# Attention decode over a long cache: scores and P V on TensorE in blocks of three pieces instead of piece by piece

## The chip, the core and the metric

The kernel runs on one core of one Trainium2 chip. The metric is the device time of one launch in microseconds (us). Most of the work is a stream of 512 MB of K and V out of HBM that TensorE (PE), VectorE (DVE) and the DMA queues share.

## The reference, cut to what matters

```python
xn = _layernorm(x)                                   # x: 4 x 1 x 512
q = (xn @ wq) -> (B=4, H=32, 1, Dh=128)
scores = einsum("bhqd,bhkd->bhqk", q, k_cache) * Dh ** -0.5   # k_cache: 4 x 32 x 8192 x 128
p = softmax(scores)
o = einsum("bhqk,bhkd->bhqd", p, v_cache)                     # v_cache: 4 x 32 x 8192 x 128
out = x + o @ wo + (silu(xn @ w_gate) * (xn @ w_up)) @ w_down
```

All tensors are bfloat16. One query per sequence meets 8192 keys in each of 128 pairs of sequence and head.

## The kernel before

The 128 pairs are cut into 32 tiles of four heads of one sequence. A tile's K and its V are 128 partitions x 32768 bf16 each (8.39 MB), and each fills one of three big buffers called slots. `load_k` (L94) and `load_v`/`v_from` (L107) issue one DMA for a whole slot on SyncE's queue (SP), and the issue waits until the slot's last reader is done. The order of all work is written out by hand, with no scheduler.

Scores of a tile come in NP = 32 pieces. For piece p, `t_piece` (L278) lets DVE transpose part of K out of the slot into a small buffer `kt`, of which there are three; `s_piece` then runs two matmuls (`sps<-kt,zq`, 128 weight columns, 512 columns streamed). After the last piece come `max_1` (L291, DVE) and `build_q` for the next tile (L269, DVE). The softmax of tile i-1 is finished inside tile i: `max_2` (L297 to L306) at piece 4, `row_sums` at piece 14, and `pt_turn` (L315), which turns the probabilities into the weights `ptz`, at piece 18. P V of a tile is 64 chunks, each one matmul `oacc<-slot,ptz` with 16 weight columns and 512 columns of V (`pv_chunk`). All these matmuls go through the helper `mm` and so carry L75.

Side by side means this: in the first half of tile i (16 pieces), P V of tile i-2 does its second 32 chunks, and in the second half P V of tile i-1 does its first 32. `pieces` yields after each piece, and the loop then calls `pv_to(n, k)`, which runs chunks until k of tile n are done. Two slots come free on the way: V of tile i-2 at the end of the first half, where `load_k(i + 1)` stands, and K of tile i at its last transpose, where `load_v(i)` stands. Every fourth tile also does `fin` of a group of heads between its last piece and the next tile's first (seven such tiles in the steady part). The last tile (n = 31) has no half of that kind: its 32 pieces run beside all 64 chunks of tile 30.

Of the kernel before, what the change touches and what calls it, by code (L numbers as in the profile page):

```python
# [15 lines left out]
def kernel(  # L16
# [61 lines left out]
    def slot():  # L78
        return slots.tile([P, SLOT], dt.bfloat16, name="slot")
# [11 lines left out]
    def load_k(n):  # L91
        j, b = divmod(n, B)
        t_ = slot()
        nc.sync.dma_start(out=t_[:], in_=A_k_cache[b, j * HT:(j + 1) * HT, :, :].rearrange("h (p t) d -> (h p) (t d)", t=T))  # L94
        k_tiles[n] = t_

    def load_v(n, parts=(T,)):
        t_ = slot()
        v_from(n, t_, 0, 0, parts)

    def v_from(n, t_, base, t0, parts):

        j, b = divmod(n, B)
        src = A_v_cache[b, j * HT:(j + 1) * HT, :, :].rearrange("h (p t) d -> (h p) (t d)", t=T)
        v_tiles[n, t0 * Dh] = (t_, base)
        for w in parts:
            nc.sync.dma_start(out=t_[:, base:base + w * Dh], in_=src[:, t0 * Dh:(t0 + w) * Dh])  # L107
            base, t0 = base + w * Dh, t0 + w
# [106 lines left out]
    def load_ffn():  # L215
        t_ = slot()
        w, w3 = EC * F, 2 * EC * F + FC * D
        nc.sync.dma_start(out=t_[:, 0:w], in_=B_w_gate.rearrange("(p c) f -> p (c f)", c=EC))
        nc.sync.dma_start(out=t_[:, w:2 * w], in_=B_w_up.rearrange("(p c) f -> p (c f)", c=EC))
        nc.sync.dma_start(out=t_[:, 2 * w:w3], in_=B_w_down.rearrange("(p c) e -> p (c e)", c=FC))  # L220
        ffn["w"] = (t_[:, 0:w].rearrange("p (c f) -> p c f", c=EC),
                    t_[:, w:2 * w].rearrange("p (c f) -> p c f", c=EC),
                    t_[:, 2 * w:w3].rearrange("p (c e) -> p c e", c=FC))

    def do_ffn():
        wg, wu, wd = ffn["w"]

        gu_ps = psM.tile([P, 2, FC * B], dt.float32, name="mps")
        for i, w in enumerate((wg, wu)):
            for fc in range(FC):  # L230
                for c in range(EC):
                    mm(gu_ps[:, i, fc * B:(fc + 1) * B], w[:, c, fc:F:FC], xnt_w[:, c, 0:B],
                       start=(i == 0 and fc == 0 and c == 0))
        eg = kt_pool.tile([P, FC * B], dt.float32, name="kt")
        nc.scalar.activation(out=eg[:], in_=gu_ps[:, 0, :], func=ACT.Exp, scale=-1.0)
        nc.vector.tensor_scalar(out=eg[:], in0=eg[:], scalar1=1.0, scalar2=None, op0=ALU.add)
        sig = kt_pool.tile([P, FC * B], dt.float32, name="kt")
        nc.vector.reciprocal(out=sig[:], in_=eg[:])
        gs = kt_pool.tile([P, FC * B], dt.float32, name="kt")
        nc.vector.tensor_tensor(out=gs[:], in0=gu_ps[:, 0, :], in1=sig[:], op=ALU.mult)  # L240
        ht = kt_pool.tile([P, FC * B], dt.bfloat16, name="kt")
        nc.vector.tensor_tensor(out=ht[:], in0=gs[:], in1=gu_ps[:, 1, :], op=ALU.mult)
        for fc in range(FC):
            for half in range(2):
                mm(yo_ps[half][0:B, :], ht[:, fc * B:(fc + 1) * B], wd[:, fc, half * DH:(half + 1) * DH], start=False)
# [18 lines left out]
    def build_q(n):  # L264
        j, b = divmod(n, B)
        for a in range(NQ):
            h = j * HT + a
            half, cg, hh = h // 16, (h % 16) // 4, h % 4
            nc.vector.tensor_copy(  # L269
                out=zq[a * QB:(a + 1) * QB, :, XO + a * QB].rearrange("p (j r) -> p r j", r=2),  # L270
                in_=qt[a * QB:(a + 1) * QB, half, :, hh * 2:hh * 2 + 2, cg * B + b])
# [17 lines left out]
    def max_1(n):  # L289
        mx = small.tile([P, 1], dt.float32, name="mx")  # L290
        nc.vector.reduce_max(out=mx[:], in_=s_ps[n][:], axis=AX.X)  # L291
        nmx[n] = mx

    def max_2(n):

        mps = psM.tile([P, 512], dt.float32, name="mps")
        nc.tensor.matmul(mps[:, 0:P], lhsT=nmx.pop(n)[:, 0:1].to_broadcast([P, P]), rhs=ident_f[:, :],  # L297
                         is_transpose=True, start=True, stop=True, skip_group_check=True)
        nm = small.tile([P, HT], dt.float32, name="nm")
        nc.vector.tensor_reduce(out=nm[:], in_=by_row(mps[:, 0:P]), axis=AX.X, op=ALU.max, negate=True)  # L300
        nc.vector.tensor_tensor(out=nm[:], in0=nm[:], in1=rowb_q[:], op=ALU.mult)  # L301
        nb = small.tile([P, 1], dt.float32, name="nb")
        nc.vector.reduce_sum(out=nb[:], in_=nm[:], axis=AX.X)
        p_ = pp.tile([P, 512], dt.bfloat16, name="p_")
        rs = small.tile([P, 1], dt.float32, name="rs")
        nc.scalar.activation(out=p_[:], in_=s_ps.pop(n)[:], func=ACT.Exp, bias=nb[:, 0:1], scale=qscale,  # L306
                             accum_out=rs[:])
        pt[n] = p_
        rs_t[n] = (rs, mps)

    def pt_turn(n):
        p_ = pt[n]
        t_ = ptz
        for y in range(HT):
            nc.vector.transpose(out=t_[y * QB:(y + 1) * QB, :, y, :, :].rearrange("p s u x -> p s (u x)"),  # L315
                                in_=p_[y * QB:(y + 1) * QB, :].rearrange("p (s w) -> p s w", s=4))
        pt[n] = t_[:].rearrange("p s y u x -> p (s y u x)")

    def row_sums(n):
        j, b = divmod(n, B)  # L320
        rs, mps = rs_t.pop(n)
        mm(mps[:, P:P + HT], rs[:, 0:1].to_broadcast([P, P]), rowb[:], start=True)
        if b == 0:
            rcp[j] = small.tile([P, HT, B], dt.float32, name="rcp")
        nc.vector.reciprocal(out=rcp[j][:, :, b], in_=mps[:, P:P + HT])  # L325
# [5 lines left out]
    def pv_chunk(n, k):  # L331
        j, b = divmod(n, B)
        w = HT * NV
        off = p_off(k)
        mm(o_acc[j % 2][b * QB:b * QB + w, :], pt[n][:, off:off + (w - 1) * QB + 1:QB],
           v_cols(n, k * 512, (k + 1) * 512), start=(k == 0))
# [18 lines left out]
    def x_tile():  # L355
        return psX.tile([P, HT, B], dt.float32, name="xps")
# [21 lines left out]

    NK = T // NV
    NP = 2 * NTG  # L380
    JL = H // HT - 1
    KM = 24
    TL = 48
# [10 lines left out]
    def pv_to(n, k):  # L394
        while pv_at[n] < k:
            pv_chunk(n, pv_at[n])
            pv_at[n] += 1

    def pieces(n, p0, p1):
        for p in range(p0, p1):  # L400
            t_piece(n, *divmod(p, 2))
            s_piece(n, *divmod(p, 2))
            yield p - p0 + 1

    def fin(n):
        nonlocal wo_ready
        j, b = divmod(n, B)
        if b == B - 1:
            fin_1(j)
            fin_q(j)  # L410
            wo_ready = (j + 1) * HT

    HP = NP // 2
    build_q(0)
    load_v(0)
    for i in range(NT - 1):

        for p in pieces(i, 0, HP):
            if i >= 3:
                pv_to(i - 2, NK // 2 + 2 * p)  # L420
            if i != 2 and i > 0:
                if p == 4:
                    max_2(i - 1)
                if p == HP - 2:
                    row_sums(i - 1)
        if i >= 3:
            load_k(i + 1)

        for p in pieces(i, HP, NP):
            if p == 2 and i > 0:  # L430
                pt_turn(i - 1)
            if i >= 2 and p > 2:
                pv_to(i - 1, (p - 2) * (NK // 2) // (HP - 2))

        if i == 0:
            load_ffn()
        elif i == 1:
            load_k(2)
        elif i == NT - 2:
            load_v(i, (T // 4,) * 4)  # L440
        else:
            load_v(i)
        max_1(i)
        build_q(i + 1)
        if i >= 3:
            fin(i - 2)
        if i == 1:
            pv_to(0, 8)
            max_2(1)
            pv_to(0, NK)  # L450
            row_sums(1)
            load_v(1)
            do_ffn()
            load_k(3)

    n = NT - 1
# [7 lines left out]
    v_from(n, t_, H * D, 0, (T // 4, T // 4))  # L464
    for p in pieces(n, 0, NP):
        if p == 4:
            pt_turn(n - 1)
        if p > 8:
            pv_to(n - 1, (p - 8) * NK // (NP - 8))
    t_ = slot()  # L470
    v_from(n, t_, 0, T // 2, (64, 32, 16, 8, 8))
    max_1(n)
# [5 lines left out]
    pv_to(n, KM)  # L478
    fin_1(JL)
    xps = x_tile()  # L480
    pv_last(xps, KM * NV, T - TL, start=True)
    fin_2(JL, xps)
    pv_last(xps, T - TL, T)
    fin_3(JL, xps)
    wo_ready = H
# [38 lines left out]
```

## Time and profile before

| | |
|---|---|
| three runs | 1495.29, 1498.81, 1510.18 us; median 1498.81 |
| the profiled execution | 1507.21 us, its span 1505.4 us, mean granted PE clock 0.931 |
| PE busy | 1242.3 us (83%) |
| DVE busy | 858.5 us (57%) |
| HBM read | 550.77 MB, 366 GB/s over the span |

A busy share says how long an engine had something in flight, not whether it was on the path that sets the end. That is read from the chain of waits and, tile by tile, from the timeline.

### The profile page before, as it was taken

How to read it: one execution, taken by the hardware profiler on the slowest of the kernel's cores; microseconds unless marked ns; L12 is line 12 of the kernel's file. 1: busy time of each engine (PE TensorE's matmuls, PEld its weight loads, DVE VectorE, ACT ScalarE, POOL GpSimd, SP SyncE). 2: the span in 40 equal slices, each digit the busy share in tenths (PEclk: the TensorE clock that was granted, in tenths of full speed). 3: DMA queues.
4: the chain of work that ended last, by engine and by line, in shares of the span. 5: the costliest groups of instructions: out<-in, count | busy, mean ns of one | idle time of the engine just before them, and what ended most of it. 6: DMA issues, size and time to landing. Idle time of an engine off the chain costs nothing.

```text
span 1505.4 us, 12238 instructions
## 1 busy us (share of the span) xinstructions
PE 1242.3 (83%) x4812; PEld 322.9 (21%) x4812; DVE 858.5 (57%) x1509; ACT 34.9 (2%) x79; POOL 3.6 (0%) x11
## 2 busy tenths in 40 slices
PE   2898878888888888878888788788897888888899
PEld 1251212211122112221112211122121211212124
DVE  4935656555565555565556555566555555555553
ACT  1000000000000000000000000000000000000000
POOL 0000000000000000000000000000000000000000
PEclk9889989999999999999999899999999889998899
DMA  9999888988897988978988789887899778898794
GB/s 418 420 435 433 352 348 363 391 362 363 363 389 337 417 363 364 391 333 361 420 347 351 309 363 418 377 347 309 363 391 420 333 305 340 387 417 347 296 414 201
DMA packets 12609, 551.55 MB, mean 366 GB/s; under 512 B 1276, under 2 KB 1800, under 8 KB 3080
## 3 DMA queue, kind: packets, MB, share of 16 engines
q1 hardware_dynamic: 12536, 550.77, 86.2%
q8 instruction: 37, 0.61, 0.1%
q14 instruction: 20, 0.16, 0.0%
q10 hardware_dynamic: 16, 0.01, 0.0%
HBM read 550.77 MB, written 0.00 MB: 366 GB/s over the span
## 4 chain that ended last, share of the span: by engine, by line
PE 60%; DMA 28%; DVE 10%; issue 2%; DVEq 0%; ACT 0%; SPq 0%
PE sps L75 29%; DMA slot<-in_A_k_cache_dram 28%; PE oacc L75 27%; DVE kt L278 5%; DVE ptz L315 2%; PE mps L75 1%; PE xps L75 1%; PE yo_ps L75 1%; PE mps L297 1%; DVE mx L291 1%; DVE o L352 0%; DVE zq L269 0%; DVE nm L300 0%; DVE rcp L325 0%; DVE nm L301 0%
## 5 line engine op out<-in xcount | busy, mean ns | idle before, releaser
L75 PE MATMUL sps<-kt,zq 128*128 128x512 bf16 x2048 | 669.6, 414 | 226.0 <-DVE kt L278 226.0
L278 DVE STREAM_TRANSPOSE kt<-slot 128x512 uint32<-128x512 uint32 x1024 | 679.6, 694 | 253.2 <-PE sps L75 209.6
L75 PE MATMUL oacc<-slot,ptz 128*16 128x512 bf16 x2008 | 630.7, 407 | 1.5 <-DMA slot<-in_A_v_cache_dram 1.5
L75 PEld LDWEIGHTS <-zq 128*128 128x128 bf16 x2048 | 141.2, 100 | 658.1 <-issue 598.1
L75 PEld LDWEIGHTS <-ptz 128*16 128x16 bf16 x2008 | 144.7, 111 | 452.1 <-issue 425.4
L300 DVE TENSOR_REDUCE nm<-mps 128x4 f32<-128x64 f32 x32 | 7.2, 225 | 131.0 <-PE mps L297 131.0
L325 DVE RECIPROCAL rcp<-mps 128x4 f32<-128x4 f32 x32 | 5.9, 185 | 115.5 <-PE mps L75 115.5
L291 DVE TENSOR_REDUCE mx<-sps 128x1 f32<-128x512 f32 x32 | 22.1, 691 | 86.1 <-PE sps L75 86.1
L75 PE MATMUL xps<-rowy,o 128*32 128x4 f32 (+1 forms) x226 | 10.5, 204 | 16.9 <-DVE o L352 16.9
L269 DVE COPY zq<-qt 32x4 bf16<-32x4 bf16 x128 | 21.2, 165 | 1.3
L75 PEld LDWEIGHTS xps<-rowy,o 128*32 128x32 f32 (+1 forms) x226 | 9.8, 154 | 20.3 <-DVE o L352 20.3
L75 PEld LDWEIGHTS <-slot 128*128 128x128 bf16 (+1 forms) x306 | 12.5, 120 | 5.7 <-DVE slot L198 2.6
L75 PEld LDWEIGHTS mps<-rowb,rs 128*128 128x128 f32 x64 | 9.6, 187 | 12.8 <-issue 12.6
L75 PE MATMUL mps<-rowb,rs 128*128 128x4 f32 x64 | 12.2, 261 | 0.0
L297 PE MATMUL mps<-ident_f,mx 128*128 128x128 f32 x32 | 10.4, 325 | 0.0
L349 ACT COPY kt<-oacc 128x512 f32<-128x512 f32 x8 | 4.7, 585 | 238.4 <-PE sps L75 228.5
L350 DVE TENSOR_TENSOR kt<-kt,rowu 128x512 f32<-128x512 f32 x8 | 5.5, 692 | 5.9 <-ACT kt L349 5.7
L372 DVE TENSOR_TENSOR otn<-xps,rcp 32x16 bf16<-32x16 f32 x28 | 4.8, 170 | 7.2 <-PE xps L75 5.2
L75 PE MATMUL yo_ps<-slot,otn 128*4 128x256 bf16 x64 | 8.3, 290 | 0.3 <-DVE otn L362 0.3
L352 DVE TENSOR_REDUCE o<-kt 128x128 f32<-128x512 f32 x8 | 8.2, 1022 | 0.3
L297 PEld LDWEIGHTS mps<-ident_f,mx 128*128 128x128 f32 x32 | 4.3, 136 | 13.2 <-issue 12.3
L75 PE MATMUL sps<-slot,xnt_w 128*32 128x512 bf16 x32 | 3.6, 630 | 4.3 <-DMA slot<-in_A_wq_dram 4.3
(148 smaller groups left out, 182.8 us busy)
## 6 DMA issues: line engine op xcount, KB each, us to landing
slot<-in_A_v_cache_dram SPq DMA_DIRECT2D x7, 2048.0 KB, 16.3
slot<-in_A_wq_dram SPq DMA_DIRECT2D x1, 4096.0 KB
slot<-in_A_wo_dram SPq DMA_DIRECT2D x1, 3584.0 KB, 23.0
slot<-in_B_w_gate_dram SPq DMA_DIRECT2D x1, 1792.0 KB, 24.2
slot<-in_B_w_up_dram SPq DMA_DIRECT2D x1, 1792.0 KB, 28.1
slot<-in_B_w_down_dram SPq DMA_DIRECT2D x1, 1792.0 KB, 32.1
slot<-in_A_v_cache_dram SPq DMA_DIRECT2D x1, 1024.0 KB, 10.5
slot<-in_A_k_cache_dram SPq DMA_DIRECT2D x32, 22.6
```

Source lines behind the costliest of these rows:

```text
L75: nc.tensor.matmul(out_ap, lhsT=lhsT, rhs=rhs, start=start, stop=True, skip_group_check=True, **kw)
L269: nc.vector.tensor_copy(out=zq[a * QB:(a + 1) * QB, :, XO + a * QB].rearrange("p (j r) -> p r j", r=2), in_=qt[a * QB:(a + 1) * QB, half, ...
L278: nc.vector.transpose(out=kt[:].bitcast(dt.uint32).rearrange("p (t r) -> p t r", r=QB), in_=src[:, :, jb, :])
L291: nc.vector.reduce_max(out=mx[:], in_=s_ps[n][:], axis=AX.X)
L297: nc.tensor.matmul(mps[:, 0:P], lhsT=nmx.pop(n)[:, 0:1].to_broadcast([P, P]), rhs=ident_f[:, :], is_transpose=True, start=True, stop=True, ...
L300: nc.vector.tensor_reduce(out=nm[:], in_=by_row(mps[:, 0:P]), axis=AX.X, op=ALU.max, negate=True)
L315: nc.vector.transpose(out=t_[y * QB:(y + 1) * QB, :, y, :, :].rearrange("p s u x -> p s (u x)"), in_=p_[y * QB:(y + 1) * QB, :].rearrange( ...
L325: nc.vector.reciprocal(out=rcp[j][:, :, b], in_=mps[:, P:P + HT])
L349: nc.scalar.copy(out=o_sb[:].rearrange("p u d -> p (u d)"), in_=o_acc[j % 2][:])
L350: nc.vector.tensor_tensor(out=o_sb[:], in0=o_sb[:], in1=rowu[:].unsqueeze(2).to_broadcast([P, NV, Dh]), op=ALU.mult)
L352: nc.vector.reduce_sum(out=o1[:], in_=o_sb[:].rearrange("p u d -> p d u"), axis=AX.X)
L372: nc.vector.tensor_tensor(out=otn[q0:q1, j * 4:j * 4 + 4, :], in0=xps[q0:q1], in1=r_[q0:q1, y, :].unsqueeze(1).to_broadcast([QB, 4, B]), o ...
```

## The change

After each piece the old code ran two or three chunks of P V. The new code does that only after each third piece (PB = 3), and then runs six or seven chunks in the first half of a tile, eight in the second half, and nine or ten in the last tile. The number of pieces, chunks and matmuls and the order of DVE's, ScalarE's and SP's instructions stay. In the first half the last chunk now stands behind piece 15 instead of 16; in the second half the first chunk stands behind piece 22 (the sixth) instead of 19 (the third); in the last tile behind piece 12 instead of 9.

```diff
+    PB = 3
     for p in pieces(i, 0, HP):
-            if i >= 3:
-                pv_to(i - 2, NK // 2 + 2 * p)
+            if i >= 3 and p % PB == 0:
+                pv_to(i - 2, NK // 2 + p * (NK // 2) // (HP - HP % PB))
...
     for p in pieces(i, HP, NP):
-            if i >= 2 and p > 2:
-                pv_to(i - 1, (p - 2) * (NK // 2) // (HP - 2))
+            if i >= 2 and p > PB and p % PB == 0:
+                pv_to(i - 1, (p - PB) * (NK // 2) // (HP - HP % PB - PB))
...
     for p in pieces(n, 0, NP):
-        if p > 8:
-            pv_to(n - 1, (p - 8) * NK // (NP - 8))
+        if p > 3 * PB and p % PB == 0:
+            pv_to(n - 1, (p - 3 * PB) * NK // (NP - NP % PB - 3 * PB))
```

PE at `max_2` in the first half of a tile, before: `kt_3444` holds piece 4 and `kt_3460` piece 5 of the scores; `ptz_129` are the weights of P V.

```order
L75 MATMUL sps_3427<-kt_3444,zq_111 128x512
L75 LDWEIGHTS ptz_129
L75 MATMUL oacc1_116<-slot_3171,ptz_129 16x512
L75 LDWEIGHTS ptz_129
L75 MATMUL oacc1_116<-slot_3171,ptz_129 16x512
L297 MATMUL mps_3450<-ident_f_106,mx_3393 128x128
L75 LDWEIGHTS zq_111
L75 MATMUL sps_3427<-kt_3460,zq_111 128x512
```

The same place after the change, where `kt_3458` is piece 5 and `kt_3462` piece 6:

```order
L75 MATMUL sps_3427<-kt_3444,zq_111 128x512
L297 MATMUL mps_3448<-ident_f_106,mx_3393 128x128
L75 LDWEIGHTS zq_111
L75 MATMUL sps_3427<-kt_3458,zq_111 128x512
L75 LDWEIGHTS zq_111
L75 MATMUL sps_3427<-kt_3458,zq_111 128x512
L75 LDWEIGHTS zq_111
L75 MATMUL sps_3427<-kt_3462,zq_111 128x512
L75 LDWEIGHTS zq_111
L75 MATMUL sps_3427<-kt_3462,zq_111 128x512
L75 LDWEIGHTS ptz_129
L75 MATMUL oacc1_116<-slot_3171,ptz_129 16x512
```

The chunks that stood ahead of `max_2` and behind piece 5 have moved behind piece 6.

PE at the end of the same first half, before: `kt_3528` is piece 16, `kt_3536` piece 17, and the second `oacc1` matmul is the last reader of the slot that `load_k` waits for.

```order
L75 MATMUL sps_3427<-kt_3528,zq_111 128x512
L75 LDWEIGHTS ptz_129
L75 MATMUL oacc1_116<-slot_3171,ptz_129 16x512
L75 LDWEIGHTS ptz_129
L75 MATMUL oacc1_116<-slot_3171,ptz_129 16x512
L75 LDWEIGHTS zq_111
L75 MATMUL sps_3427<-kt_3536,zq_111 128x512
```

The same place after the change, where `kt_3530` is piece 16:

```order
L75 MATMUL oacc1_116<-slot_3171,ptz_129 16x512
L75 LDWEIGHTS ptz_129
L75 MATMUL oacc1_116<-slot_3171,ptz_129 16x512
L75 LDWEIGHTS zq_111
L75 MATMUL sps_3427<-kt_3530,zq_111 128x512
L75 LDWEIGHTS zq_111
L75 MATMUL sps_3427<-kt_3530,zq_111 128x512
L75 LDWEIGHTS zq_111
L75 MATMUL sps_3427<-kt_3536,zq_111 128x512
```

The slot's last reader now stands ahead of piece 16.

## Rows read from the trace of the kernel before

**Rows 1.** The page's part 4: the chain that ended last, by engine.

```profile
PE 60%; DMA 28%; DVE 10%; issue 2%; DVEq 0%; ACT 0%; SPq 0%
```

**Rows 2.** Timeline of SP: start us, duration us, then the DMA issued (28 L94 rows, 166.96 to 1414.93).

```profile
166.96 0.33 SPq L94 DMA_DIRECT2D slot<-in_A_k_cache_dram  x1
...
439.77 0.33 SPq L94 DMA_DIRECT2D slot<-in_A_k_cache_dram  x1
...
713.66 0.33 SPq L94 DMA_DIRECT2D slot<-in_A_k_cache_dram  x1
731.74 0.33 SPq L107 DMA_DIRECT2D slot<-in_A_v_cache_dram  x1
759.54 0.33 SPq L94 DMA_DIRECT2D slot<-in_A_k_cache_dram  x1
...
1176.27 0.33 SPq L94 DMA_DIRECT2D slot<-in_A_k_cache_dram  x1
...
1414.93 0.33 SPq L94 DMA_DIRECT2D slot<-in_A_k_cache_dram  x1
```

**Rows 3.** Chain of waits in order of time: start us, us, what it ran through.

```profile
418.36 0.72 DVE kt L278
...
459.16 0.69 DVE mx L291
...
900.65 21.71 DMA slot<-in_A_k_cache_dram
```

**Rows 4.** Timeline, all engines, 713 to 760: start, us, engine, [idle before <-releaser].

```profile
713.56 1.08 PE L75 MATMUL sps<-kt,zq 128*128 128x512 bf16 x4
...
722.18 0.63 PE L75 MATMUL sps<-kt,zq 128*128 128x512 bf16 x2
...
722.84 0.71 DVE L278 STREAM_TRANSPOSE kt<-slot 128x512 uint32<-128x512 uint32 x1 [0.69 <-PE sps L75]
...
725.16 0.62 PE L75 MATMUL oacc<-slot,ptz 128*16 128x512 bf16 x2
...
725.71 0.62 PE L75 MATMUL sps<-kt,zq 128*128 128x512 bf16 x2
...
726.26 0.83 PE L75 MATMUL oacc<-slot,ptz 128*16 128x512 bf16 x3
...
727.03 0.62 PE L75 MATMUL sps<-kt,zq 128*128 128x512 bf16 x2
...
736.70 2.49 DVE L278 STREAM_TRANSPOSE kt<-slot 128x512 uint32<-128x512 uint32 x4 [0.86 <-DMA slot<-in_A_k_cache_dram]
```

**Rows 5.** Timeline of tile 1: P V with no scores in between.

```profile
83.46 12.27 PE L75 MATMUL oacc<-slot,ptz 128*16 128x512 bf16 x56
```

**Rows 6.** The page's part 5, weight loads: count | busy us, mean ns | idle before.

```profile
L75 PEld LDWEIGHTS <-zq 128*128 128x128 bf16 x2048 | 141.2, 100 | 658.1 <-issue 598.1
L75 PEld LDWEIGHTS <-ptz 128*16 128x16 bf16 x2008 | 144.7, 111 | 452.1 <-issue 425.4
```

**Rows 7.** Timeline of PE, 396 to 490: the piece after `pt_turn`.

```profile
443.49 0.61 PE L75 MATMUL sps<-kt,zq 128*128 128x512 bf16 x2 [2.75 <-DVE kt L278]
```

**Rows 8.** Windows: length, busy of PE, PEld, DVE, ACT, POOL, PEclk, DMA share, GB/s.

```profile
740.00:741.00 1.00, 1.00 (x3) 0.13 (x2) 0.00 (x0) 0.00 (x0) 0.00 (x0) 0.50 0.45 197
...
759.00:760.00 1.00, 1.00 (x5) 0.33 (x5) 0.38 (x1) 0.00 (x0) 0.00 (x0) 1.00 0.00 0
...
100.00:150.00 50.00, 41.05 (x191) 14.35 (x190) 28.09 (x49) 0.22 (x1) 0.00 (x0) 0.86 1.01 435
```

**Rows 9.** Timeline, start of another tile, after a longer wait of PE.

```profile
1152.40 2.53 DVE L278 STREAM_TRANSPOSE kt<-slot 128x512 uint32<-128x512 uint32 x4 [2.81 <-DMA slot<-in_A_k_cache_dram]
1153.16 1.01 PE L75 MATMUL sps<-kt,zq 128*128 128x512 bf16 x2 [4.16 <-DVE kt L278]
```

**Rows 10.** Timelines of PE and of DVE, last tile: piece 5 on, and its maximum.

```profile
1450.06 4.42 PE L75 MATMUL sps<-kt,zq 128*128 128x512 bf16 x10 [2.86 <-DVE kt L278]
...
1483.80 0.69 DVE L291 TENSOR_REDUCE mx<-sps 128x1 f32<-128x512 f32 x1 [3.03 <-PE sps L75]
```

## The prediction

> **What bounds the kernel now.** I read the chain of waits first. PE holds 60% of it and DMA 28% [rows 1], so neither alone is the bound, and the question is where each sits. SP's timeline answers that: a tile's beat is the time from one K issue to the next, and the 28 steady issues give (1414.93 - 166.96) / 27 = 46.2 us [rows 2]. The reader should lay one beat out. K for the next tile is issued at 713.66, when PE has read the last chunk of the old V; it lands at 736.70, where DVE's first transpose had waited for nothing else [rows 2, 4]. That is 23.0 us; the shortest load on the chain took 21.7 [rows 3]. Then comes the first half of the new tile, 736.70 to 759.54, 22.8 us, at whose end the last P V chunk frees the slot for the next K. So the beat is K's load plus a first half on PE. The second half runs inside K's load and the V load inside the first half; both have slack. In the last microsecond before the K issue at 759.54 the DMA moved nothing [rows 8], so it is PE that holds the transfer back there, not bandwidth. At the best rate seen, 435 GB/s [rows 8], K and V of a tile (2 x 8.39 MB) need 38.6 us, well under 46.2.
>
> In seven tiles of the 28, the ones with a `fin`, the second half is longer than K's load and takes its place in the beat. In five others there is no wait for K either, but by fractions of a microsecond.
>
> What PE pays within a half: a pair of score matmuls and a pair of P V chunks take turns and each pair costs 0.55 us, 725.16 to 725.71 to 726.26 [rows 4]. A third chunk in a row adds only 0.77 - 0.55 = 0.22, and a run of 56 chunks cost 12.27 / 56 = 0.22 each [rows 4, 5]. Two further score matmuls in a row add 1.08 - 0.62 = 0.46, so 0.23 each [rows 4]. A piece with two chunks, 1.10 us, is thus 0.23 + 0.22 for the second of each pair and 0.65 for the two turns from one kind to the other. If a turn cost no more than a matmul in a run, those 0.65 would be 0.45.
>
> **The change, part by part.** *First half.* The turns go from 16 rounds to 5. Before: 16 pieces with two chunks, 16 x 1.10 = 17.6 us. After, a block of three pieces and six chunks is 5 x 0.23 + 5 x 0.22 + 0.65 = 2.90 us; five of them and two more chunks are 14.9, and K's issue no longer stands behind piece 16. That is 2.7 less. Against it: the first three pieces of a tile have no chunks between them, so DVE paces them, at 2.49 / 4 = 0.62 a piece [rows 4] instead of the 0.46 that PE needs, 2 x 0.16 = 0.3. After `max_2` DVE starts afresh behind its small reductions, which PE waits for now as then; but piece 6 follows piece 5 without chunks between, another 0.16. `row_sums` stalls PE as before. Net 2.2 us a half, and 28 halves give 62 us.
>
> *Can DVE feed the blocks?* It may start a transpose when a `kt` buffer is read: it started 0.66 us after the piece's first matmul (722.18 to 722.84) and took 0.71 [rows 4]. In a block starting at 0 the three buffers come free at about 0.66, 1.12 and 1.58, the transposes end by 1.4, 2.0 and 2.6, and PE wants the first at 2.90. So it costs nothing, with 0.3 us of cover for the third and 1.5 for the first.
>
> *Second half.* Up to piece 19 nothing moves: PE waits for `pt_turn` as before. From piece 19 to the maximum the trace has 443.49 to 459.16, 15.7 us [rows 3, 7]. After: pieces 19 to 22 at DVE's pace 3 x 0.62 = 1.9, piece 22 with eight chunks and two turns 0.23 + 7 x 0.22 + 0.65 = 2.4, three blocks of three pieces and eight chunks 3 x 3.34 = 10.0, and 0.7 from piece 32's start to the maximum: 15.0. The 0.7 saved counts in the seven `fin` tiles, 5 us, and in part in the five without a wait, 2 us; in the other sixteen K's load covers it and PE only waits longer.
>
> *Last tile.* Piece 5 to the maximum is 1450.06 to 1483.80, 33.7 us, of which five pieces ran at 4.42 / 5 = 0.88 [rows 10]. After: seven pieces at 0.88, 6.2; piece 12 with nine chunks 2.6; five blocks with nine chunks 17.8; one with ten 3.8; pieces 31 and 32 with the way to the maximum 1.1: 31.5. With the second half ahead of it, 3 us.
>
> *Clock.* This is where the change can lose. [...] A deeper fall is on record: after 4.16 us of waiting the clock was low from the first matmul, and the half ran from 1152.40 to 1176.27, 23.9 [rows 2, 9]. If twenty more halves did that it would cost 20 x 1.0 = 20 us. Bounds 0 and 20; I take 0, because the low stretch falls on pieces that DVE now paces, where it costs 0.88 - 0.62 = 0.26 a piece; two scores and two chunks at half the clock would lose up to 4 x 0.22.
>
> *Sum.* 62 + 5 + 2 + 3 - 7 = 65 us. The profiled execution took 1507.2 (span 1505.4) and would take 1442; it lies 8 us above the median of the three runs, 1498.8, and from there I forecast **1434 us**, 4.3% less.
>
> [...]
>
> **Rivals.** *DVE starves the blocks (slower).* Three buffers, three pieces: if DVE could refill only behind the block's chunks, at about 2.6 us, the first piece would be ready at 3.3 and the next two 0.62 apart, so the next block's scores would end at 3.3 + 1.24 + 0.46 = 5.0 instead of 2.90 + 3 x 0.46 = 4.3, 0.7 a block and 3.5 a half. From 2.2 / 5 = 0.44 a block on the kernel is slower; at 0.7 it is 28 x 1.3 = 36 us slower, 1535. Against it: the start 0.66 after the first matmul of a piece. 4%.
>
> *The DMA takes the gain (no change).* If the loads ran no faster than today's average, K would land later by what the first half saves, and the beat would stay at 46.2: 1499. For it: the beat would fall to 43.9, of which 38.6 is the floor. Against it: the idle DMA ahead of a K issue. 5%.
>
> *Weight loads come into the open (slower).* The loads take 0.10 and 0.11 us [rows 6]. A first half has 25 gaps between two scores and 27 between two chunks: 25 x 0.10 + 27 x 0.11 = 5.5 us, against the 2.2 gained, 3.3 x 28 = 92 us, 1591. Against it: 0.22 and 0.23 in runs of 56 and 4 leave no room for a load in the open. 2%.
>
> *The clock falls deeper.* With the 20 us above, 45 us are left, 1454; still faster. 8%.
>
> **How the numbers follow.** The forecast has 80%, and with the clock's rival 88% lie below 1484. A measurement of this kernel can tell about 1% from no change; 6% is within it, 5 for the DMA and 1 for a mixture, and 6% slower. The range takes the clock's 20 us and another 10 for prices read too well (0.01 us in a matmul of a run is 0.5 us a half, 15 in all) at the high end: 1464. At the low end K's loads may come down to the 21.7 of the shortest, about 1 us in sixteen tiles, and the five halves may keep their clock, with some more from the runs: 31 us, 1403.
>
> **What would show it.** The timeline of the changed kernel should have runs of six score matmuls and of six to eight chunks, a block of 2.9 us in the first half, no wait of PE for DVE inside such a block, and the three waits at `max_2`, `row_sums` and `pt_turn` as before. From K's landing to the next K issue it should take 19 to 21 us, from a K issue to the landing 22 to 23, and the beat 43 to 44. PE's wait ahead of a tile should grow, and the granted clock be low at the start of nearly every tile. I am wrong if the runs of scores cost more than 0.25 a matmul, if DVE's starts come behind the chunks, if the low clock lasts past `max_2`, or if K's load grows by what the half gains.

## The result, and the profile after

The changed kernel takes 1423.12 us (median; 1421.55 to 1424.33) against 1498.83: ratio 0.948, 95% interval [0.943, 0.953], 76 us less. The forecast was 1434. The profiled execution took 1422.08.

The page of the changed kernel: span, busy time, and the chain that ended last by engine.

```profile
span 1420.3 us, 12185 instructions
...
PE 1120.2 (79%) x4730; PEld 425.3 (30%) x4812; DVE 822.0 (58%) x1509; ACT 34.9 (2%) x79; POOL 3.6 (0%) x11
...
PE 50%; DMA 36%; DVE 10%; issue 3%; another core or an unknown queue 1%; DVEq 0%; ACT 0%; SPq 0%
```

PE's share of the chain fell from 60% [rows 1] to 50% and the DMA's rose from 28% to 36%: the beat is still K's load plus a first half on PE, but the second term shrank. Some score matmuls have no record in this trace (1966 of 2048 have one), so that a run of six can show as five; whether the 1% of the chain under "another core or an unknown queue" comes of that is open.

SP's timeline, first and last steady K issue and one beat:

```profile
163.54 0.33 SPq L94 DMA_DIRECT2D slot<-in_A_k_cache_dram  x1
...
381.74 0.33 SPq L94 DMA_DIRECT2D slot<-in_A_k_cache_dram  x1
398.93 0.33 SPq L107 DMA_DIRECT2D slot<-in_A_v_cache_dram  x1
422.51 0.33 SPq L94 DMA_DIRECT2D slot<-in_A_k_cache_dram  x1
...
1336.22 0.33 SPq L94 DMA_DIRECT2D slot<-in_A_k_cache_dram  x1
```

The mean beat is (1336.22 - 163.54) / 27 = 43.4 us, against 46.2 [rows 2]. PE's timeline in the first half that ends at 422.51, one whose clock stayed up (its first transpose began at 403.72):

```profile
404.48 1.80 PE L75 MATMUL sps<-kt,zq 128*128 128x512 bf16 x6 [3.02 <-DVE kt L278]
406.21 1.48 PE L75 MATMUL oacc<-slot,ptz 128*16 128x512 bf16 x6
407.62 0.62 PE L75 MATMUL sps<-kt,zq 128*128 128x512 bf16 x2
408.09 0.27 PE L297 MATMUL mps<-ident_f,mx 128*128 128x128 f32 x1
409.68 1.20 PE L75 MATMUL sps<-kt,zq 128*128 128x512 bf16 x4 [1.32 <-DVE kt L278]
410.81 1.48 PE L75 MATMUL oacc<-slot,ptz 128*16 128x512 bf16 x6
412.23 1.52 PE L75 MATMUL sps<-kt,zq 128*128 128x512 bf16 x5
413.68 1.70 PE L75 MATMUL oacc<-slot,ptz 128*16 128x512 bf16 x7
415.31 1.53 PE L75 MATMUL sps<-kt,zq 128*128 128x512 bf16 x6
416.77 1.48 PE L75 MATMUL oacc<-slot,ptz 128*16 128x512 bf16 x6
418.18 1.07 PE L75 MATMUL sps<-kt,zq 128*128 128x512 bf16 x4
```

A block of three pieces and six chunks runs from 415.31 to 418.18, 2.87 us, with no wait inside it; piece by piece, three pieces took three times 1.10 [rows 4]. The half is 422.51 - 403.72 = 18.8 us, against 21.4 for the same kind before [rows 2, 3].

Most halves are not of that kind. The windows of a first half that began with a low clock (columns as in [rows 8]) and the first row of PE in it:

```profile
319.00:321.00 2.00, 2.00 (x6) 0.58 (x4) 1.56 (x3) 0.00 (x0) 0.00 (x0) 0.50 1.21 524
321.00:323.00 2.00, 2.00 (x6) 0.55 (x5) 0.00 (x0) 0.00 (x0) 0.00 (x0) 0.50 1.21 524
404.00:406.00 2.00, 1.52 (x6) 0.48 (x5) 2.00 (x4) 0.00 (x0) 0.00 (x0) 1.00 1.21 524
```

```profile
318.80 2.72 PE L75 MATMUL sps<-kt,zq 128*128 128x512 bf16 x6 [2.83 <-DVE kt L278]
```

The granted clock is 0.50 there and 1.00 at 404; the half with the low clock took 21.3 us. Of the 28 halves 3 kept their clock, that is, it stayed at 1.00 from the first transpose to the K issue (5 before).

### The profile page after: what moved, and what is told of

Same layout as the page of the kernel before. It is cut to its first block, busy times and chain, and to the rows that moved or that the text cites. A ratio compares the mean times of both kernels' runs of the same rounds, so it can differ in the third digit from the quotient of the medians.

```text
span 1420.3 us, 12185 instructions
## 1 busy us (share of the span) xinstructions
PE 1120.2 (79%) x4730; PEld 425.3 (30%) x4812; DVE 822.0 (58%) x1509; ACT 34.9 (2%) x79; POOL 3.6 (0%) x11
## 4 chain that ended last, share of the span: by engine, by line
PE 50%; DMA 36%; DVE 10%; issue 3%; another core or an unknown queue 1%; DVEq 0%; ACT 0%; SPq 0%
DMA slot<-in_A_k_cache_dram 36%; PE sps L75 24%; PE oacc L75 23%; DVE kt L278 5%; DVE ptz L315 1%; PE xps L75 1%; PE yo_ps L75 1%; PE mps L75 1%; DVE o L352 1%; DVE nm L300 0%; DVE rcp L325 0%; DVE mx L291 0%; PE mps L297 0%; DVE nm L301 0%
## 5 line engine op out<-in xcount | busy, mean ns | idle before, releaser
L278 DVE STREAM_TRANSPOSE kt<-slot 128x512 uint32<-128x512 uint32 x1024 | 643.2, 682 | 268.8 <-PE sps L75 170.1
L75 PE MATMUL sps<-kt,zq 128*128 128x512 bf16 x1966 | 591.0, 418 | 257.4 <-DVE kt L278 253.5
L75 PE MATMUL oacc<-slot,ptz 128*16 128x512 bf16 x2008 | 515.2, 401 | 0.5 <-issue 0.5
L75 PEld LDWEIGHTS <-zq 128*128 128x128 bf16 x2048 | 187.1, 102 | 612.4 <-issue 426.4
L75 PEld LDWEIGHTS <-ptz 128*16 128x16 bf16 x2008 | 194.3, 109 | 317.5 <-issue 169.5
L75 PE MATMUL xps<-rowy,o 128*32 128x4 f32 (+1 forms) x226 | 10.7, 205 | 22.9 <-DVE o L352 22.9
L75 PE MATMUL mps<-rowb,rs 128*128 128x4 f32 x64 | 9.3, 215 | 0.1
L75 PE MATMUL mps<-xnt_w,slot 128*128 128x4 bf16 x112 | 6.8, 199 | 0.3 <-DVE rcp L325 0.3
## 6 DMA issues: line engine op xcount, KB each, us to landing
slot<-in_B_w_gate_dram SPq DMA_DIRECT2D x1, 1792.0 KB, 23.7
```

The source lines that it names most:

```text
L75: nc.tensor.matmul(out_ap, lhsT=lhsT, rhs=rhs, start=start, stop=True, skip_group_check=True, **kw)
L278: nc.vector.transpose(out=kt[:].bitcast(dt.uint32).rearrange("p (t r) -> p t r", r=QB), in_=src[:, :, jb, :])
```

## The experiments

Each beat below is read as in the result: "half" is the time from a tile's first transpose to the next K issue (a mean half is over all 28), "reach" the time from a K issue to the next tile's first transpose, in the twenty steady tiles without `fin` unless said otherwise.

**Which half.** Blocks in one half alone.

```diff
 e1_first_half: the new pv_to in the first half; second half and last tile as before
 e2_second_half: the new pv_to in the second half; first half and last tile as before
```

> Blocks of three pieces in the first half of a tile alone; second half and last tile as before. If the gain comes from fewer turns between scores and P V in the first half, which stands on the beat: nearly all of it, 28 halves x 2.3 us = 64, so 1430 to 1440. If both halves share the gain: about 1461. If the gain comes from the second half (V issued earlier): 1490 to 1499.

Measured 1427.33 us, ratio 0.949 [0.946, 0.953], 3 under the first expectation. The halves that kept their clock took 18.8, the mean half 20.1 (22.9 before).

> Blocks in the second half of a tile alone. If K's load covers the second half in most tiles: only the seven fin tiles (0.9 us each) and the five without a wait gain, less any clock lost to PE's longer wait: 1487 to 1499. If both halves share the gain: about 1461.

Measured 1505.86, ratio 1.003 [1.000, 1.005]: nothing gained, and 7 above the expectation. The second half did get shorter, but reach stayed at 22.6 (22.6 before), since K's load covers it; in the seven `fin` tiles it fell from 25.4 to 24.5. What that gave, the clock took: none of the 28 halves kept it, mean granted clock 0.904 against 0.931, mean half 23.1 against 22.9. So nearly the whole gain sits in the first half, and the same blocks in the second half are worth nothing by themselves.

**Turns or place.** The old order with the last chunk ahead of piece 16.

```diff
-            if i >= 3:
-                pv_to(i - 2, NK // 2 + 2 * p)
+            if i >= 3 and p < HP:
+                pv_to(i - 2, NK // 2 + p * (NK // 2) // (HP - 1))
```

> The old turn-taking piece by piece, but the 32 chunks of the first half spread over 15 pieces, so that the last one stands ahead of piece 16 as in the change. If only the turns count: one round less, 16 x 1.10 - 15 x 1.10 - 2 x 0.22 = 0.66 us a half, 18 us, 1480. If the earlier place of the last chunk (and of K's issue) is the gain: 1430 to 1440.

Measured 1481.52, ratio 0.986 [0.982, 0.990]. A half that kept its clock took 20.7, 0.7 less: piece 16, its two score matmuls and its turns, now stands behind the K issue. The earlier K issue is thus a quarter of the gain (19 of 76 us); the rest comes of the blocks.

**What makes a turn dear.** The order of before, with P V matmuls of full width.

```diff
-        mm(o_acc[j % 2][b * QB:b * QB + w, :], pt[n][:, off:off + (w - 1) * QB + 1:QB],
+        mm(o_acc[j % 2][:, :], pt[n][:, (k % 16) * P:(k % 16 + 1) * P],
```

> The kernel before, with P V matmuls that load 128 weight columns and write all 128 rows of the accumulator instead of 16 at one 32-row place; the result of P V is not the attention's, the streamed bytes are the same. If a turn costs because the matmuls change between a full-width and a narrow weight tile: a pair goes from 0.55 to 0.45 us with the order of before, a first half from 21.4 to about 18.5, and the kernel to 1400 to 1430. If a turn costs because the streamed tile or the accumulator bank changes: pairs stay at 0.55 and the kernel at 1499 within 1%.

Measured 1390.27, ratio 0.924 [0.920, 0.928], 10 under the expectation, which priced the first halves alone: the reach of the `fin` tiles fell too, from 25.4 to 22.8. None of the 28 halves kept its clock. PE's timeline, still piece by piece:

```profile
659.77 0.61 PE L75 MATMUL sps<-kt,zq 128*128 128x512 bf16 x2
660.22 0.59 PE L75 MATMUL oacc<-slot,ptz 128*128 128x512 bf16 x2
660.65 0.61 PE L75 MATMUL sps<-kt,zq 128*128 128x512 bf16 x2
```

A piece with two chunks takes 0.88 us (659.77 to 660.65) instead of 1.10: four matmuls at 0.22, and a turn costs no more than a matmul in a run. What a turn is made of can be read from the weight loads (PEld). Two of them in the kernel before, then two in this run:

```profile
725.16 0.14 PEld L75 LDWEIGHTS <-ptz 128*16 128x16 bf16 x2 [0.44 <-issue]
725.71 0.11 PEld L75 LDWEIGHTS <-zq 128*128 128x128 bf16 x2 [0.41 <-issue]
```

```profile
660.00 0.32 PEld L75 LDWEIGHTS <-ptz 128*128 128x128 bf16 x2
660.44 0.31 PEld L75 LDWEIGHTS <-zq 128*128 128x128 bf16 x2
```

Before, the first load of a kind starts together with its own matmul (725.16 and 725.71, the times of PE's rows in [rows 4]), 0.31 us after the last matmul of the other kind began (the 0.55 of a pair less the 0.24 between its two). In this run it starts 0.22 ahead of its matmul (660.00 for the one at 660.22), beside the running scores. So at the turns between the two widths the weight load did not go ahead, and what the turn cost over a matmul in a run, 0.31 - 0.22 = 0.09 us, is about one load (0.10 and 0.11 [rows 6]). Why it did not go ahead there is not shown.

The wide run changed two things, the width and the layout of the weights, so the next one changes the layout alone.

```diff
+        mm(o_acc[j % 2][b * QB:b * QB + w, :], pt[n][:, (k % 16) * P:(k % 16) * P + w],
```

> The kernel before, with P V's 16 weight columns taken from 16 neighbouring elements instead of 16 elements 32 apart, written to the same 32-row place; the result of P V is not the attention's. If the turn costs because the weight tile is narrow: pairs stay at 0.55 us and the kernel at 1499 within 1%. If it costs because the strided weight load cannot be prefetched at a turn (the wide run changed that too): pairs at 0.45, 1385 to 1400.

Measured 1491.19, ratio 0.993 [0.990, 0.995]. PE's timeline:

```profile
658.08 0.62 PE L75 MATMUL sps<-kt,zq 128*128 128x512 bf16 x2
658.63 0.60 PE L75 MATMUL oacc<-slot,ptz 128*16 128x512 bf16 x2
659.16 0.62 PE L75 MATMUL sps<-kt,zq 128*128 128x512 bf16 x2
```

1.08 a piece: 0.02 of the 0.22 was the layout, the rest is the change between a full-width weight tile and a narrow one in a 32-row place. Which of the four places it was made no difference: the four sequences of a group write to different ones, and a turn was 0.31 to 0.32 in all four, here and in the kernel before.

**Block size.**

```diff
-    PB = 3
+    PB = 2     (e5_pb2)
+    PB = 4     (e6_pb4)
```

> Blocks of two pieces (PB = 2) everywhere. By turns: a block of two pieces and four chunks is 3 x 0.23 + 3 x 0.22 + 0.65 = 2.0 us, eight of them 16.0 against 17.6 with the last chunk behind piece 16; less 0.2 for DVE's pace, 1.4 a half, 39 us: 1455 to 1465. If DVE starved blocks of three, blocks of two would do as well or better than 1423.

Measured 1444.09, ratio 0.963 [0.960, 0.967], better than expected by 11. The half that kept its clock took 20.0, 1.4 less than before, as worked out. The expectation had left out the `fin` tiles, whose reach fell from 25.4 to 23.7 (12 us over seven), and the last tile (5 us).

> Blocks of four pieces (PB = 4) with three kt buffers; the last chunk stands behind piece 16 again. By turns: four pieces and eight chunks are 7 x 0.23 + 7 x 0.22 + 0.65 = 3.8, four of them 15.2, so 0.3 more than the change's first half, and 0.3 for DVE's pace: 1423 to 1445. If a block longer than the buffers starves: another 0.7 a block, 2.8 a half, above 1490.

Measured 1435.65, ratio 0.958 [0.955, 0.961], within the first expectation. PE's timeline shows a block of four pieces, one more than there are buffers, without a wait:

```profile
681.14 2.04 PE L75 MATMUL sps<-kt,zq 128*128 128x512 bf16 x7
683.11 1.91 PE L75 MATMUL oacc<-slot,ptz 128*16 128x512 bf16 x8
684.95 1.08 PE L75 MATMUL sps<-kt,zq 128*128 128x512 bf16 x4
```

681.14 to 684.95 is 3.81 us for four pieces and eight chunks, the 3.8 worked out. That three is the better size here would follow from the sums, since 15 pieces let K's issue go ahead of piece 16; it was not tried by itself. The one half that kept its clock took 19.7, 0.9 over the change's, where the sums made 0.6.

**DVE's feed.** The change with two `kt` buffers.

```diff
-    kt_pool = ctx.enter_context(tc.tile_pool(name="ktp", bufs=3))
+    kt_pool = ctx.enter_context(tc.tile_pool(name="ktp", bufs=2))
```

> The change with two kt buffers instead of three. If three buffers are what feeds a block of three: the third piece's transpose starts 0.66 us into the block and ends at 1.4 where PE wants it at 0.9, 0.4 to 0.5 a block, 2 to 2.5 us a half on the beat: 1480 to 1495. If DVE had slack beyond that: 1423 within 1%.

Measured 1512.09, ratio 1.007 [1.005, 1.010]: worse than expected, and slower than before. PE's and DVE's timeline in a first half:

```profile
674.08 1.08 PE L75 MATMUL sps<-kt,zq 128*128 128x512 bf16 x4
674.74 2.12 DVE L278 STREAM_TRANSPOSE kt<-slot 128x512 uint32<-128x512 uint32 x3 [1.48 <-PE sps L75]
675.50 0.61 PE L75 MATMUL sps<-kt,zq 128*128 128x512 bf16 x2 [0.35 <-DVE kt L278]
```

PE waits 0.35 us for the third piece of a block, a little under the expected 0.4 to 0.5, and the half that keeps its clock is 20.0, 1.2 over the change's 18.8 and not 2 to 2.5. What was left out of the expectation is the second half: it too slowed, and reach went from 22.6 to 24.3, past K's load (in the `fin` tiles from 24.1 to 27.7). The starving of the blocks is real at two buffers and absent at three.

**The low clock.** 16 matmuls more per tile behind the last piece, into the bank that the next tile's first score matmul overwrites.

```diff
+    def warm(n, count):
+        s_ps[n] = psS.tile([P, 512], dt.float32, name="sps")
+        z_ = ptz[:].rearrange("p s y u x -> p (s y u x)")
+        for k in range(count):
+            mm(s_ps[n][:], z_[:, 0:P], z_[:, 512:1024], start=True)
...
         max_1(i)
+        if i >= 3:
+            warm(i + 1, 16)
```

> The change, and 16 matmuls of 512 columns more per tile behind the last piece, into the next scores' bank, where the first real matmul overwrites them; they fill 3.5 us of PE's wait for K. If 25 of 28 first halves lose 1.3 to 2.5 us to the low clock after that wait: they fall from 20.5 to about 19, and the kernel to 1375 to 1395. If the low clock is not caused by the wait, or K's load takes up what the half gains: 1415 to 1425; if the extra matmuls delay the next tile: above 1423.

Measured 1386.70, ratio 0.925 [0.923, 0.928], the fastest version here with the whole computation, 36 us under the change. PE's and DVE's timeline around K's landing:

```profile
855.60 0.63 PE L75 MATMUL sps<-kt,zq 128*128 128x512 bf16 x2
856.07 3.61 PE L75 MATMUL sps<-ptz 128*128 128x512 bf16 x16
...
858.59 2.49 DVE L278 STREAM_TRANSPOSE kt<-slot 128x512 uint32<-128x512 uint32 x4 [1.01 <-DMA slot<-in_A_k_cache_dram]
859.52 1.63 PE L75 MATMUL sps<-kt,zq 128*128 128x512 bf16 x6
```

27 of the 28 halves now take 18.8 to 18.9 us, mean 18.85 against 20.44, and the granted clock is 0.966 against 0.921. Reach grew by 0.2 in the tiles without `fin`. A window over one whole beat:

```profile
795.64:836.50 40.86, 36.00 (x145) 13.73 (x148) 24.88 (x45) 0.78 (x2) 0.00 (x0) 0.96 0.97 411
```

At this beat of 40.9 us the DMA's busy share is 0.97, against 38.6 us that K and V would take at 435 GB/s [rows 8]. That little is left for a change on PE is a guess from there; no run tried it.

> The kernel before, with the same 16 matmuls per tile. PE waits 2.2 to 4.2 us for K there, so in part of the tiles they run over it and push the next tile's first scores back by up to 1 us, against 1.4 us of low clock saved in 23 of 28 halves: 1470 to 1490. If the clock counts for nothing: 1499 to 1525.

Measured 1498.97, ratio 0.999 [0.997, 1.000]; the clock is 0.964, 21 of the 28 halves keep it, and still nothing is gained, 9 above the first expectation. PE's and DVE's timeline after a short wait:

```profile
560.96 3.63 PE L75 MATMUL sps<-ptz 128*128 128x512 bf16 x16
561.65 1.90 DVE L278 STREAM_TRANSPOSE kt<-slot 128x512 uint32<-128x512 uint32 x3
564.43 0.61 PE L75 MATMUL sps<-kt,zq 128*128 128x512 bf16 x2
```

K's first transpose began at 561.65 there and its scores could have started 0.8 us later (1152.40 to 1153.16 in [rows 9]); they started at 564.43, 2.0 late. PE's wait ahead of a tile without `fin` is 1.4 to 4.2 us before and 2.8 to 5.8 in the change: mostly too short for 3.6 us of extra work before, so the same lines pay only together with the blocks. I had priced the delay at up to 1 us.

**Full width with the right columns.** The order of before; the 16 wanted columns lie side by side, P V takes 128 neighbouring columns into a bank of its tile's own, rows 0 to 15 are kept, and `fin_1` runs per tile on 16 rows.

```diff
+        mm(o_acc[n % 2][:], pt[n][:, off:off + P], v_cols(n, k * 512, (k + 1) * 512), start=(k == 0))
...
+            nc.vector.transpose(out=ptv[y * QB:(y + 1) * QB, :, y, :, :],
+                                in_=p_[y * QB:(y + 1) * QB, :].rearrange("p (s u x) -> p s u x", s=4, u=NV))
```

> The order of before, piece by piece, with P V on 128 neighbouring weight columns of which the first 16 rows of the result are kept: the probabilities are laid out with the 16 wanted columns side by side, each tile has an accumulator bank of its own, and fin's copy, product and sum run per tile on 16 rows. If the width makes the turn's price: first halves as in the wide run, 19 to 20, and the extra 2 us of DVE per tile lie in the wait for K: 1385 to 1405. If pt_turn's write with a stride or the copies come onto the beat: above 1410.

Measured 1572.66, ratio 1.048 [1.044, 1.052]. DVE's and PE's timeline at `pt_turn`:

```profile
699.47 9.27 DVE L313 STREAM_TRANSPOSE ptz<-p__3488 32x512 bf16<-32x512 bf16 x4 [0.31 <-PE oacc L74]
...
708.77 2.52 DVE L277 STREAM_TRANSPOSE kt<-slot 128x512 uint32<-128x512 uint32 x4
709.53 1.01 PE L74 MATMUL sps<-kt,zq 128*128 128x512 bf16 x2 [9.27 <-DVE kt L277]
```

The same four in the kernel before:

```profile
439.85 2.85 DVE L315 STREAM_TRANSPOSE ptz<-p__2308 32x512 bf16<-32x512 bf16 x4 [0.65 <-PE oacc L75]
```

Four transposes that write with a step of 16 elements take 9.27 us, against 2.85 before, and PE waits for all of it. Reach becomes 28.2 where K's load takes 22.4. The first half itself is 17.8 where the clock held, 1.0 under the change's, so the width did what it should and the layout cost more.

> The same with 24 matmuls more per tile in PE's wait for K (5.2 us of 5.9 to 7.4). If the low clock is the rest of the loss: first halves 17.3 to 17.8, K 22.6, a beat of 40.0 to 40.4: 1325 to 1345. If the DMA is the next bound (38.6 us for K and V at 435 GB/s and what it takes to start): K's load grows and the beat stays at 41 to 42, 1360 to 1390.

Measured 1597.44, ratio 1.065 [1.061, 1.068]: neither expectation. With reach bound by DVE and PE there is no wait for K to fill, and the 24 matmuls stand in the way: reach is 28.5, and in the `fin` tiles 32.6 instead of 30.1. What a full-width P V with a cheap layout would give is not shown.

## Why the prediction was right, point by point

*What bounds the kernel.* Right: the beat is K's load plus the first half. Blocks in the first half alone give 1427, in the second half alone nothing.

*First half, 62 us.* The mechanism was right and the size low. A half that keeps its clock fell by 21.4 - 18.8 = 2.6 us, not 2.2, which is 73 us over 28. The block was priced at 2.90 and takes 2.87, 0.15 over five; 16 pieces were rounded down to 17.6 from 17.68; and I had let the two stalls stay as they were. PE's timeline of the kernel before, at `max_2` and at `row_sums` of the half in [rows 3]:

```profile
423.54 0.32 PE L297 MATMUL mps<-ident_f,mx 128*128 128x128 f32 x1
425.18 0.61 PE L75 MATMUL sps<-kt,zq 128*128 128x512 bf16 x2 [1.32 <-DVE kt L278]
436.22 0.38 PE L75 MATMUL mps<-rowb,rs 128*128 128x4 f32 x2
437.48 0.61 PE L75 MATMUL sps<-kt,zq 128*128 128x512 bf16 x2 [0.87 <-DVE kt L278]
```

The weight load at `max_2` and PE at `row_sums` in the changed kernel:

```profile
407.86 0.13 PEld L297 LDWEIGHTS mps<-ident_f,mx 128*128 128x128 f32 x1
...
419.09 0.28 PE L75 MATMUL mps<-rowb,rs 128*128 128x4 f32 x2
420.24 0.61 PE L75 MATMUL sps<-kt,zq 128*128 128x512 bf16 x2 [0.87 <-DVE kt L278]
```

From the small matmul to the next score it is 1.64 at `max_2` there and 409.68 - 408.09 = 1.59 now; at `row_sums` 1.26 there and 1.15 now. Behind full-width scores the small matmul's weights are loaded ahead of it (407.86 for 408.09); behind P V their load starts together with it (423.54), as at the other turns. Together these make the 0.4.

*DVE can feed the blocks.* Right: no wait inside a block with three buffers, 0.35 us with two. The rival of the starved blocks is out for this kernel; with two buffers its mechanism is there, and the kernel is slower than before.

*Second half, 5 + 2 us.* Reach in the `fin` tiles fell from 25.4 to 24.1, 9 us over seven; in the others from 22.62 to 22.56, 1 us over twenty. Right in kind, but the saving of a `fin` tile was put too low, 0.7 for 1.3. The trace of before has four tiles without a wait for K and not five.

*Last tile, 3 us.* From the last K issue to the end of the span it was 1505.4 - 1414.93 = 90.5 [rows 2] and is 1420.3 - 1336.22 = 84.1: 6 us. I had let seven pieces keep the low clock's 0.88; the row below has eight pieces in 5.5 us, 0.69 each, with a granted clock of 0.69 (window 1368.48 to 1374) where the five pieces of before had 0.50 (window 1450.06 to 1454.48). Nothing in the prediction foresaw that, so this part of the gain, about 1 us, is luck.

PE's timeline in the last tile, piece 5 to 12, and DVE's at the maximum:

```profile
1368.48 5.52 PE L75 MATMUL sps<-kt,zq 128*128 128x512 bf16 x16 [2.86 <-DVE kt L278]
...
1398.43 0.69 DVE L291 TENSOR_REDUCE mx<-sps 128x1 f32<-128x512 f32 x1 [2.87 <-PE sps L75]
```

*Clock, -7 us.* The 7 were five halves at 1.4 us, the same five as in the range. Before, 5 of the 28 halves kept their clock and took 21.4, as 418.36 to 439.77 [rows 2, 3]; the one from 736.70, whose granted clock was 0.50 at 740 [rows 8], took 22.8. No run shows the 7 by itself; nearest is `e2_second_half`, whose first halves have the code of before: none kept its clock, and the mean half was 23.1 against 22.9, 6 us over 28. Near, for the change: the mean half lies 1.65 us over one that kept its clock, against 1.48 before, 5 us over 28. The halves that begin low are 25, not 28. The deeper fall (21.3 us) came too, in about half of them, but costs 2.5 over the undisturbed 18.8, as the 23.9 did over 21.4.

*Sum.* Halves 28 x 2.44 = 68, `fin` tiles 9, others 1, last tile 6: 84 us between the two profiled executions, which differ by 85.1. The forecast's terms made 65 and were thus 20 short there, 11 short on the medians; the profiled execution of before lay 8 us above its median, which the forecast had taken off. How much of the 20 belongs to that one execution is open.

*Weight loads in the open, the third rival.* Out for a run of one kind: in blocks a matmul comes each 0.22 to 0.23 us, and each has a load of 0.10 to 0.11 of its own. The loads of the block at 415.31 in the result:

```profile
415.31 1.02 PEld L75 LDWEIGHTS <-zq 128*128 128x128 bf16 x6 [0.42 <-issue]
416.77 0.99 PEld L75 LDWEIGHTS <-ptz 128*16 128x16 bf16 x6 [0.44 <-issue]
```

The sixth load has ended 1.02 us after the first began, and the sixth matmul starts 5 x 0.23 = 1.15 in; for the narrow tiles it is 0.99 and 5 x 0.22 = 1.10. So in this block the load goes beside the matmul ahead of its own, for full-width and for narrow tiles. The load in the open that the rival feared is there, but at a turn between the two widths (0.09 us over a matmul in a run), and the blocks save it.

*The DMA's rival.* K's load did not grow by what the half gained: reach is 22.6 before and after. With the clock held up the DMA's share of a beat came to 0.97 and reach grew by 0.2; whether the DMA bounds the kernel then was not tried. Why single K loads take anything from 21.8 to 23.5 us was not tried and stays open.

## What to carry to other kernels

When two kinds of matmul alternate on PE, compare the marginal cost of one more of a kind (0.22 to 0.23 us here) with the cost of a pair (0.55); if a pair costs more than two of these, run each kind in blocks, check that the buffers that feed them suffice (PE waited 0.35 us in a block with two, not at all with three), and look whether one kind can be given the other's weight width (0.88 instead of 1.10 a piece). The longest block need not be the best: three pieces took 1423 us, two 1444 and four 1436. Do it first where PE stands on the beat of the transfers; in the stretch that a transfer covered it bought only a longer wait (1505.86 in `e2_second_half`), and there the clock fell from 0.931 to 0.904. Such a wait can be filled with matmuls whose result is overwritten, but only where it is longer than they are: 3.6 us of them gained 36 us over the change's waits of 2.8 to 5.8, and nothing over those of 1.4 to 4.2 before.

## What the runs showed of the hardware that I had not expected

- A round of two turns between weight tiles of 128 and of 16 columns cost 0.20 to 0.22 us over matmuls in a run (1.10 for four matmuls); between two tiles of 128 columns it cost nothing (0.88 for four matmuls in `e4_wide_pv`), with the streamed tile and the accumulator bank changing all the same. In the first case the weight load started together with its matmul (725.16), in the second 0.22 ahead of it (660.00 for 660.22).
- A DVE transpose of 32x512 bf16 took 2.3 us when it wrote with a step of 16 elements (9.27 for four, `e10_true_wide`) and 0.7 with neighbouring ones (2.85 for four, before).
- The length of PE's wait alone did not decide the clock: after 2.83 us the next half of the change began at 0.50 of full (318.80), after 3.02 us at 1.00 (404.48). What else decides it is not shown.
